# One core: the first products of two sequence blocks write half their planes straight into the sum, and the other half is added by accumulating DMA

## Chip, cores and metric

The kernel runs on one core of one Trainium2 chip. The metric is the device time of one execution in microseconds; the median of the runs of the kernel before is 262.36 (three runs, 262.0 to 262.48).

## What is computed

Inputs are bf16, the sequence has 2048 positions and 640 channels. `_A_ref` is a gated long convolution, `_B_ref` a SwiGLU feed-forward network with 1728 hidden units.

```python
def _A_ref(q, k, v, shift_k, ssm_k, ssm_D):
    # k_shift: sum over 4 taps of shifted k times shift_k
    kv = k_shift * v
    # y: causal convolution of kv with ssm_k over the 2048 positions, per channel
    y = y + kv * ssm_D
    return q * y

def _B_ref(x, w_gate, w_up, w_down):
    return (silu(x @ w_gate) * (x @ w_up)) @ w_down

h = x + _A_ref(layernorm(x), k, v, shift_k, ssm_k, ssm_D)
h2 = h + _B_ref(layernorm(h), w_gate, w_up, w_down)
```

## The kernel before

The sequence is cut into four blocks i of 512 positions. The convolution is done with a transform over 512 points with real and imaginary planes, written as matmuls against a table `ftab`. For each block of the filter, `kload` fetches it (`kc`), `ktrans` turns it on TensorE and evicts it to `KT`, and `kfwd` transforms it (L613) into even and odd parts (`C`, `R` and `KO`), which VectorE joins by a sum and a difference (`bfly`, L584). `kcomb` adds neighbours: on VectorE for C1 (L695), by accumulating DMA from GpSimd for the two others (L691).

For a block of the input, `kv` fetches k transposed (`kT`, a DMA transpose, L517) and v (`vt`), makes the shifted sum on TensorE (L715, L720), evicts it into `kT`, brings it back by five DMA transposes into `kvo`, and VectorE multiplies it into `vt` (L751). For block 0 the way back is by TensorE (L734, L739). `xfwd` transforms `vt` (L613; block 2 uses `quarters`, L650) into `X` and `FO`; `kvo` lies in the same bytes as `FO`, so the transposes into `kvo` wait until the last butterfly has read `FO`.

`prod(j, i)` multiplies the transform of input block j with filter part i - j and adds it to the sum `Y` of output block i. For each half f2 there are two multiplications over 2560 elements per partition (L826, L827), which write four planes into the ring `T` of five slots; one subtraction and one addition over 1280 elements (L832) make of them the real and the imaginary result. For j = 0 these two write `Y` itself; for j > 0 they write `T` and a third instruction adds that to `Y` (L843), except for the products (1,3) and (2,3), whose results go to `ZB` and are added to `Y` by a DMA that GpSimd issues (L840, `accum_op`). With j = i a last butterfly makes `IE` and `IO`. `IO` lies in the bytes of `vt`, so the next load of `vt` waits until the inverse transform has read `IO`.

`inverse(i)` transforms back (L907, four tiles of PSUM, two from `IO` and two from `IE`), and for each tile VectorE multiplies by the normalized q and forms a sum (L921, into `xh`), GpSimd scales it (L925), ScalarE forms the sum of squares (L927) and adds epsilon (L951), GpSimd takes the power -1/2 (L958), and ScalarE (L961, L963; VectorE, L966, in block 0) writes the normalized tile `qo`. A DMA transpose on SP's queue turns it into `hnT`. `ffn(i)` needs `hnT`: gate and up products are L1030 and L1031, or L988 in blocks 0 and 3, which work on halves of `hnT` and so start after two of the four transposes. ScalarE evicts both (L1006, L1008 or L1053, L1055; `GU`, `ub`), VectorE multiplies them (L1010, L1057); the down projection is L1093, with short remainders at L1105 and L1075. The results are added to `xh` (L1120, L1123, L1082) and stored.

PSUM is used as four units of two banks; a tile of matmuls waits until one is free, which is when an eviction (`evict`, L505 on ScalarE, L495 and L497 on VectorE) has read it. What order the instructions have on each of the five engines is written out by hand: `ORDER` lists the numbers of all tasks for each engine (a task is one instruction or one group of matmuls), `VECTOR` the evictions that VectorE takes instead of ScalarE, `FILL` some extra matmuls. `schedule` only fits the lists together and picks the PSUM units; each engine runs its list in order and waits on semaphores where a task needs another. So an instruction that waits holds back all that stands behind it on its engine.

Of the kernel before, what the change touches and what calls it, by code (L numbers as in the profile page):

```python
# [10 lines left out]
ALU = mybir.AluOpType  # L11
# [12 lines left out]
class _Task:  # L24
    __slots__ = ("eng", "fn", "cost", "lat", "deps", "after", "succ", "npred", "ready", "end", "start",
                 "opens", "tiles", "idx", "clock", "sem", "seq", "dma", "name", "gap", "lock", "fill", "late", "pause", "alt")
# [32 lines left out]
class _Graph:  # L59
# [38 lines left out]
    def add(self, eng, name, fn, cost, r=(), w=(), pr=(), pw=(), skip=(), lat=None, dma=None, after=(), lock=None):  # L98
        t = _Task()
# [11 lines left out]
        t.alt = None  # L111
        t.seq = len(self.tasks)
        for ap in r:
            for c in self.cells(ap):
                q = self.lastw.get(c)
# [3 lines left out]
        for ap in w:  # L119
            for c in self.cells(ap):  # L120
                q = self.lastw.get(c)
# [109 lines left out]
    def emit(self, block):  # L231
# [5 lines left out]
        for t in self.glob:  # L237
# [13 lines left out]
            for d in (t.deps | {t.pause} if t.pause is not None else t.deps):  # L251
                if d.eng == t.eng == "pe":
                    continue
                key = d.sem if d.dma is not None else d.eng
                val = 16 if d.dma is not None else d.idx
                merged.append((d, key, val))
# [13 lines left out]
            if t.dma is not None:  # L270
                t.sem = es.enter_context(nc.semaphore("s_d%d" % nd))
                nd += 1
                t.clock[t.sem] = 16
# [4 lines left out]
        for t in self.glob:  # L278
            if t.dma is not None and not t.succ:
                prog["sp"].append(lambda e, t=t: e.wait_ge(t.sem, 16))  # L280
# [49 lines left out]
    """,  # L330
    "dve": """
# [874 lines left out]
```

## Time and profile before

| | |
|---|---|
| median of 3 runs | 262.36 us |
| the profiled execution | 261.95 us |
| its span | 260.1 us |
| TensorE matmul busy | 253.6 us, 97% |
| VectorE busy | 203.3 us, 78%, 298 instructions |
| ScalarE busy | 188.4 us, 72% |
| GpSimd busy | 35.8 us, 14% |

All durations below come from that one execution; its time lies 1.85 us above its span, which is the time before the first and after the last instruction. In the profile PE is TensorE, PEld its weight loads, DVE is VectorE, ACT ScalarE, POOL GpSimd and SP the queue that issues most DMAs. A row of the timeline gives start, duration, engine, line, what is written from what, and in brackets how long the engine had stood idle and what ended that. Neighbouring instructions of an engine overlap a little, so that the distance from one start to the next is shorter than the duration. In the chain of waits each row is a piece of the chain of work that ended last. Matmuls overlap so much that PE shows as busy also where it is merely spread out; whether it waited is read from the distance between starts.

### The profile page before, as it was taken

How to read it: one execution, taken by the hardware profiler on the slowest of the kernel's cores; microseconds unless marked ns; L12 is line 12 of the kernel's file. 1: busy time of each engine (PE TensorE's matmuls, PEld its weight loads, DVE VectorE, ACT ScalarE, POOL GpSimd, SP SyncE). 2: the span in 40 equal slices, each digit the busy share in tenths (PEclk: the TensorE clock that was granted, in tenths of full speed). 3: DMA queues.
4: the chain of work that ended last, by engine and by line, in shares of the span. 5: the costliest groups of instructions: out<-in, count | busy, mean ns of one | idle time of the engine just before them, and what ended most of it. 6: DMA issues, size and time to landing. Idle time of an engine off the chain costs nothing.

```text
span 260.1 us, 4707 instructions
## 1 busy us (share of the span) xinstructions
PE 253.6 (97%) x1900; PEld 168.4 (65%) x1900; DVE 203.3 (78%) x298; ACT 188.4 (72%) x359; POOL 35.8 (14%) x53
## 2 busy tenths in 40 slices
PE   8999988899999999999999999999999999999996
PEld 6767545468888757644445667444456678888763
DVE  1799899999999999999999999999998131123214
ACT  2789999995996889668978697548698846745320
POOL 1000400401213033000040170311003202000000
DMA  6998964999999771630110064794500020300003
GB/s 186 327 346 223 326 161 84 227 317 217 228 135 178 96 195 28 151 126 5 40 20 0 12 154 104 177 215 89 103 1 0 4 50 25 79 0 3 25 3 126
DMA packets 44793, 31.13 MB, mean 120 GB/s; under 512 B 32354, under 2 KB 41443, under 8 KB 44771
## 3 DMA queue, kind: packets, MB, share of 16 engines
q1 hardware_dynamic: 41968, 25.58, 37.8%
q0 software_dynamic: 2144, 5.24, 11.7%
q8 instruction: 15, 0.25, 0.4%
q10 hardware_dynamic: 658, 0.01, 0.1%
q14 instruction: 8, 0.06, 0.1%
HBM read 15.69 MB, written 2.62 MB: 70 GB/s over the span
## 4 chain that ended last, share of the span: by engine, by line
PE 86%; ACT 6%; DVE 4%; DMA 2%; issue 1%; SPq 0%; DVEq 0%
PE ps L988 22%; PE ps L1093 20%; PE ps L1030 11%; PE ps L1031 11%; PE ps L613 7%; PE ps L907 6%; PE ps L720 3%; DMA kc<-in_A_ssm_k_dram 2%; ACT C L505 1%; PE ps L1075 1%; ACT KT L505 1%; PE ps L1105 1%; PE ps L715 1%; DVE xh L921 1%; ACT KO L505 1%; ACT X L505 1%
## 5 line engine op out<-in xcount | busy, mean ns | idle before, releaser
L1093 PE MATMUL ps<-Wd,GU 128*128 128x384 bf16 (+1 forms) x390 | 55.5, 299 | 0.0
L1093 PEld LDWEIGHTS ps<-Wd,GU 128*128 128x128 bf16 x390 | 37.9, 98 | 15.7 <-issue 0.9
L988 PE MATMUL ps<-hnT,GA 128*128 128x256 bf16 x140 | 31.1, 273 | 0.0
L988 PE MATMUL ps<-hnT,UA 128*128 128x256 bf16 x140 | 31.1, 273 | 0.0
L826 DVE TENSOR_TENSOR T<-X,C 128x2560 bf16<-128x2560 bf16 x20 | 29.7, 1485 | 0.2
L827 DVE TENSOR_TENSOR T<-X,C 128x2560 bf16<-128x2560 bf16 x20 | 29.7, 1483 | 0.1
L1010 DVE TENSOR_TENSOR GU<-GU,ub 128x512 bf16<-128x512 bf16 (+1 forms) x28 | 10.8, 401 | 21.3 <-ACT ub L1008 17.5
L988 PE MATMUL ps<-hnT,UB 128*128 128x256 bf16 x120 | 26.9, 273 | 0.0
L988 PE MATMUL ps<-hnT,GB 128*128 128x256 bf16 x120 | 26.9, 272 | 0.0
L1030 PE MATMUL ps<-hnT,GA 128*128 128x512 bf16 x70 | 26.5, 379 | 0.0
L1031 PE MATMUL ps<-hnT,UA 128*128 128x512 bf16 x70 | 26.5, 379 | 0.0
L1008 ACT ACTIVATE ub<-ps 128x512 bf16<-128x512 f32 (+2 forms) x32 | 17.0, 540 | 9.9 <-DVE GU L1010 3.8
L1006 ACT ACTIVATE GU<-ps 128x512 bf16<-128x512 f32 (+1 forms) x28 | 15.1, 562 | 10.8 <-PE ps L988 10.6
L1030 PE MATMUL ps<-hnT,GB 128*128 128x512 bf16 x60 | 22.8, 379 | 0.0
L1031 PE MATMUL ps<-hnT,UB 128*128 128x512 bf16 x60 | 22.7, 379 | 0.0
L613 PE MATMUL ps<-KT,ftab 128*128 128x320 bf16 x128 | 20.1, 300 | 1.4 <-ACT kT L505 0.6
L1053 ACT ACTIVATE GU<-ps 128x512 bf16<-128x512 f32 x26 | 15.1, 598 | 7.4 <-PE ps L1031 7.4
L1055 ACT ACTIVATE ub<-ps 128x512 bf16<-128x512 f32 (+1 forms) x30 | 16.8, 569 | 5.0 <-DVE GU L1057 4.0
L878 POOL TENSOR_TENSOR st<-st,half 128x8 f32<-128x8 f32 x4 | 9.6, 2400 | 74.9 <-ACT st L872 74.9
L921 DVE SCALAR_TENSOR_TENSOR xh<-ps,st,xh 128x640 bf16<-128x640 f32 x16 | 13.6, 880 | 6.8 <-PE ps L907 5.7
L927 ACT ACTIVATE qo<-xh,mv 128x640 bf16<-128x640 bf16 x16 | 13.3, 828 | 6.9 <-POOL mv L925 6.9
L613 PEld LDWEIGHTS ps<-KT,ftab 128*128 128x128 bf16 x128 | 10.8, 98 | 9.3 <-ACT KT L505 1.4
(108 smaller groups left out, 492.8 us busy)
## 6 DMA issues: line engine op xcount, KB each, us to landing
kc<-in_A_ssm_k_dram SPq DMA_DIRECT2D x4, 640.0 KB, 6.4
xh<-in_A_q_dram SPq DMA_DIRECT2D x4, 640.0 KB, 5.3
vt<-in_A_v_dram SPq DMA_DIRECT2D x4, 640.0 KB, 4.3
Y<-ZB POOLq DMA_DIRECT2D x4, 640.0 KB, 5.7
out_dram<-xh SPq DMA_DIRECT2D x15, 160.0 KB, 1.9
Wd<-in_B_w_down_dram SPq DMA_DIRECT2D x1, 1280.0 KB, 8.9
C<-C POOLq DMA_DIRECT2D x1, 1280.0 KB, 11.4
C<-R POOLq DMA_DIRECT2D x1, 1280.0 KB, 11.2
```

The source lines that it names most:

```text
L613: last = e.matmul(pt.f(c, W), ftab[:, cs, j, f * P:(f + 1) * P], src[:, j, c * W:(c + 1) * W], start=(j == par), stop=(j == par + 2))
L826: g.add("dve", nm, lambda e, x=x, k=k, t1=t1: e.tensor_tensor(out=t1, in0=x, in1=k, op=ALU.mult), cdve(2560), r=[x, k], w=[t1])
L827: g.add("dve", nm, lambda e, x=x, k=ksw, t2=t2: e.tensor_tensor(out=t2, in0=x, in1=k, op=ALU.mult), cdve(2560), r=[x, k], w=[t2])
L907: last = e.matmul(pt.f(c, W), itab[:, cs, f, j, :], src[:, j // 2 if len(fs) == 1 else f, cs, c * W:(c + 1) * W], start=(f == 0 and cs == ...
L921: g.add("dve", nm, lambda e, pt=pt, x2=x2, s=s, j=j, m=m: e.scalar_tensor_tensor(out=x2, in0=pt.f2(W), scalar=s[:, 3, j:j + 1], in1=x2, op ...
L988: last = e.matmul(pt.flat(M, a + M * k), w[:, c, f0:f0 + P], hnT[:, c, ts], start=(c == 0), stop=(c == NC5 - 1))
L1006: g.add("act", nm, lambda e, pt=pt, gv=gv, pg=pg: e.activation(out=gv, in_=pg(pt), func=ACTF.Silu, scale=gain), max(400, cact(n)), w=[gv], ...
L1008: g.add("act", nm, lambda e, pt=pt, uv=uv, pu=pu: e.activation(out=uv, in_=pu(pt), func=ACTF.Copy, scale=gain), max(400, cact(n)), w=[uv], ...
L1030: e.matmul(pt.f(0, N), wg[:, c, f0:f0 + P], hnT[:, c, :], start=(c == 0), stop=(c == NC5 - 1))
L1031: last = e.matmul(pt.f(1, N), wu[:, c, f0:f0 + P], hnT[:, c, :], start=(c == 0), stop=(c == NC5 - 1))
L1055: g.add("act", nm, lambda e, pt=pt, uv=uv, a=ps_u, ts=ts: e.activation(out=uv, in_=pt.f(a[0], N, a[1])[:, ts], func=ACTF.Copy, scale=gain) ...
L1093: last = e.matmul(pt.flat(c1 - c0, P + c0), slots[fb][:, at * P:(at + 1) * P], Wd[:, fb, c0:c1], start=(fb == 0 and not second), stop=(fb ...
```

## The change

Two products, (0,2) and (0,3), go through the function `planes`, which was there and was called by nothing. `YT` is one tensor over the bytes of `Y`, what lies between, and `T`, so that one instruction can write a plane into `Y` and its partner into `T`. Of each product half, the two multiplications (L823) write planes 0 and 2 (for odd i 1 and 2) into `Y` and the two others into `T`; one instruction negates one of them in `T` (L826 in the changed file, a `tensor_scalar` over 1280 elements); and GpSimd issues one accumulating DMA (L833) that adds the two planes in `T` to the two in `Y`, 2 x 1280 elements per partition. The subtraction and addition (L832 before) fall away. `VECTOR` changes: VectorE evicts one `KT` tile and two `KO` tiles at the start (before: two `KT` and one `R`), and two more tiles late, one `kT` of block 3 and one `X` of block 3. And `ORDER` is a new list for all engines: the whole program stands in another order.

```diff
-        BN, ..., ACC, EA, KD, RD, LA, RA, HALF, PL = ..., (0, 1, 2), (0, 3), ()
+        BN, ..., ACC, EA, KD, RD, LA, RA, HALF, PL, TK, TE = ..., (0, 1, 2), (0, 3), ((0, 2), (0, 3)), (), 'pool'
...
-        Y = sb("Y", S[6], [2, 2, 2, D])
...
-        T = sb("T", o, [NU, 2, D])
+        YT = sb("YT", S[6], [(T_END - S[6]) // 2])
+        Y = YT[:, 0:8 * D].rearrange("p (f c s d) -> p f c s d", f=2, c=2, s=2)
+        T = YT[:, (T_OFF - S[6]) // 2:(T_END - S[6]) // 2].rearrange("p (u f d) -> p u f d", u=NU, f=2)
...
         def at_big(off, *dims):
-            return bass.AP(BIG[:].tensor, BIG[:].offset + off // 2, [list(BIG[:].ap[0])] + [list(d) for d in dims])
+            b, at = (BIG, 0) if off < S[6] else (BZ, S[7]) if S[7] <= off < S[7] + SLOT else (YT, S[6])
+            return bass.AP(b[:].tensor, b[:].offset + (off - at) // 2, [list(b[:].ap[0])] + [list(d) for d in dims])
...
 VECTOR = """
-    36 59 83
+    33 85 87 710 758
 """
```

`TK` is empty, so the new branch in `kload` and `ktrans` is not taken. The function that is now called, for j = 0:

```python
un = [ring_t.pop(0) for _ in range(2)]
ring_t.extend(un)
a, b = (T_OFF + 2560 * v for v in un)
u = [a, yo[1], yo[0], b] if i % 2 else [yo[0], a, yo[1], b]
neg = u[0] if i % 2 else u[1]
# for each pair of planes: d = x * k over u[p], u[q]; after the first pair: z = -z on plane neg
sets = ((3, 0),) if i % 2 else ((1, 3),)
# for each set: accumulating DMA from GpSimd, Y += the two planes in T
```

Three places show what moved. On VectorE, in block 1's inverse transform, the product (0,2) stood in this order (`X_54` is the transform of block 0, `C_51` the filter part 2, `xh_73` block 1's tile):

```order
L826 TENSOR_TENSOR T<-X_54,C_51 128x2x2x640
L827 TENSOR_TENSOR T<-X_54,C_51 128x2x2x640
L1010 TENSOR_TENSOR gz<-gz,ub_78 64x256
L921 SCALAR_TENSOR_TENSOR xh_73,mv_107<-ps,st_1_106,xh_73 128x640
L832 TENSOR_TENSOR Y<-T 128x1280
L1010 TENSOR_TENSOR GU<-GU,ub_78 128x256
L826 TENSOR_TENSOR T<-X_54,C_51 128x2x2x640
L751 TENSOR_TENSOR vt<-vt,kvo 128x4x3x128
L751 TENSOR_TENSOR vt<-vt,kvo 128x4x2x64
L832 TENSOR_TENSOR Y<-T 128x1280 x2
L827 TENSOR_TENSOR T<-X_54,C_51 128x2x2x640
```

Now it stands so (L947 is what L921 was, block 1's tile is `xh_72`, L1036 was L1010, L775 was L751):

```order
L823 TENSOR_TENSOR YT<-X_54,C_51 128x2x2x640
L1036 TENSOR_TENSOR gz<-gz,ub_77 64x256
L826 TENSOR_SCALAR YT<-YT 128x1280
L947 SCALAR_TENSOR_TENSOR xh_72,mv_107<-ps,st_1_105,xh_72 128x640
L947 SCALAR_TENSOR_TENSOR xh_72,mv_109<-ps,st_1_105,xh_72 128x640
L823 TENSOR_TENSOR YT<-X_54,C_51 128x2x2x640 x2
L1036 TENSOR_TENSOR GU<-GU,ub_77 128x256
L947 SCALAR_TENSOR_TENSOR xh_72,mv_106<-ps,st_1_105,xh_72 128x640
L823 TENSOR_TENSOR YT<-X_54,C_51 128x2x2x640
L1036 TENSOR_TENSOR GU<-GU,ub_78 128x2x256
L826 TENSOR_SCALAR YT<-YT 128x1280
L947 SCALAR_TENSOR_TENSOR xh_72,mv_108<-ps,st_1_105,xh_72 128x640
```

The four L832 are gone, two negations have come, and the multiplications of the product have moved in among the four per-tile steps of the inverse transform, three of which stood ahead of them before. On GpSimd, in the same place, the accumulating DMAs stand between the steps of the second layer norm (L951 was L925, L984 was L958):

```order
L951 TENSOR_SCALAR mv_109<-mv_109 128x1
L951 TENSOR_SCALAR mv_107<-mv_107 128x1
L833 DMA YT<-YT 128x2x1280
L984 TENSOR_TENSOR mv_107<-mv_107,half 128x1
L951 TENSOR_SCALAR mv_106<-mv_106 128x1
L984 TENSOR_TENSOR mv_109<-mv_109,half 128x1
L833 DMA YT<-YT 128x2x1280
L951 TENSOR_SCALAR mv_108<-mv_108 128x1
L984 TENSOR_TENSOR mv_106<-mv_106,half 128x1
L984 TENSOR_TENSOR mv_108<-mv_108,half 128x1
```

Before there was no DMA in that stretch; in block 2 two more stand in the same way. On SP's queue, in block 1's `kv`, the table of the inverse transform was fetched ahead of the transposes into `kvo`:

```order
L512 DMA GA<-in_B_w_gate_dram 128x5x896
L512 DMA itab<-cst_itab 128x2048
L517 DMA_TRANSPOSE kvo<-kT 128x4x128
L512 DMA PK<-in_B_w_up_dram 128x5x64
L517 DMA_TRANSPOSE kvo<-kT 128x4x128
L512 DMA PK<-in_B_w_gate_dram 128x5x64
L517 DMA_TRANSPOSE kvo<-kT 128x4x128 x3
L512 DMA vt<-in_A_v_dram 128x2560
```

Now the table comes behind the first of these transposes, and other weights come earlier:

```order
L515 DMA Wd<-in_B_w_down_dram 64x640
L515 DMA xh_72<-in_A_q_dram 128x2560
L515 DMA GB<-in_B_w_gate_dram 128x5x768
L520 DMA_TRANSPOSE kvo<-kT 128x4x128
L515 DMA itab<-cst_itab 128x2048
L520 DMA_TRANSPOSE kvo<-kT 128x4x128 x4
L515 DMA vt<-in_A_v_dram 128x2560
```

The order of the rest has changed as follows where the steps below need it. On ScalarE, up to the eviction that frees the PSUM unit for the first inverse tile of block 0, there are now 7 `KT` and 1 short `kT` eviction where there were 6 and 2, with 32 of 640 elements and 4 long `kT` in both; the first long `kT` eviction of block 1 stands behind 7 `KT` evictions instead of 4. On TensorE, the first ten transposes of one filter block are now followed by ten of the other, instead of twenty and twenty. In block 2, the matmuls between the last tile of the inverse transform and the first gate product are 52 of the down projection, 32 transform matmuls of block 3 (L613 before) and 4 remainders; before, they were 78, 20 and 8. Both programs have the same matmuls in all.

More of the change, by code (lines that the diff above doesn't have):

```diff
@@ L25 @@
     __slots__ = ("eng", "fn", "cost", "lat", "deps", "after", "succ", "npred", "ready", "end", "start",
-                 "opens", "tiles", "idx", "clock", "sem", "seq", "dma", "name", "gap", "lock", "fill", "late", "pause", "alt")
+                 "opens", "tiles", "idx", "clock", "sem", "seq", "dma", "name", "gap", "lock", "fill", "late", "pause", "alt", "parts")
 class _Tile:
@@ L111, in add @@
         t.alt = None
+        t.parts = 1
         t.seq = len(self.tasks)
@@ L254, in emit @@
                 key = d.sem if d.dma is not None else d.eng
-                val = 16 if d.dma is not None else d.idx
+                val = 16 * d.parts if d.dma is not None else d.idx
                 merged.append((d, key, val))
@@ L272, in emit @@
                 nd += 1
-                t.clock[t.sem] = 16
+                t.clock[t.sem] = 16 * t.parts
                 prog[t.eng].append(lambda e, t=t: t.fn(e).then_inc(t.sem, 16))
@@ L279, in emit @@
             if t.dma is not None and not t.succ:
-                prog["sp"].append(lambda e, t=t: e.wait_ge(t.sem, 16))
+                prog["sp"].append(lambda e, t=t: e.wait_ge(t.sem, 16 * t.parts))
         @block.gpsimd
@@ L318 @@
     "act": """
[11 rows of a table removed]
[11 rows of a table added]
     """,
     "dve": """
[10 rows of a table removed]
[10 rows of a table added]
     """,
     "pool": """
-        8 6 5 7 10 11 9 151 209 195 216 212 202 198 219 205 134 135 339 417 401 409 420 393 412 396 404 528 613 605 597 621
-        616 608 624 600 771 776 781 786 732 822 825 806 809 814 830 817 833
+        10 8 6 7 5 11 9 151 216 195 209 198 202 212 219 205 134 135 339 417 401 563 404 393 420 567 409 396 412 528 621 742
+        624 613 746 605 616 597 608 600 771 776 781 786 732 806 830 822 825 833 809 814 817
     """,
     "sp": """
[3 rows of a table removed]
[3 rows of a table added]
     """,
@@ L451, in bass_sequential_preLN__ssm_conv_h3__swiglu_ffn__prompt_kernel @@
         o += 17920
+        GB_OFF = o
         GB = sb("GB", o, [NC5, FBK * P])
@@ L470, in bass_sequential_preLN__ssm_conv_h3__swiglu_ffn__prompt_kernel @@
         assert o + 576 <= SBB + 16481 - A0, o + 576
-        BN, DIRECT, D8, PT, BN2, ST, R4, PAIR, WARM, ACC, EA, KD, RD, LA, RA, HALF, PL = (0,), (), (), (0,), (), (0, 1, 2, 3), ('xf2',), True, 24, ((1, 3), (2, 3)), True, (2, 3), (), (1, 2, 3), (0, 1, 2), (0, 3), ()
+        BN, DIRECT, D8, PT, BN2, ST, R4, PAIR, WARM, ACC, EA, KD, RD, LA, RA, HALF, PL, TK, TE = (0,), (), (), (0,), (), (0, 1, 2, 3), ('xf2',), True, 24, ((1, 3), (2, 3)), True, (2, 3), (), (1, 2, 3), (0, 1, 2), (0, 3), ((0, 2), (0, 3)), (), 'pool'
         g = _Graph(nc, es)
@@ L558, in bass_sequential_preLN__ssm_conv_h3__swiglu_ffn__prompt_kernel, with move @@
               r=[wcol[:], ident[:]], w=[dl[:]])
+        box = {}
         def kload(m):
+            if m in TK:
+                q = sb("kq%d" % m, (GB_OFF, GB_OFF + 10240, kc23, kc23 + 5120)[m], [4, D])
+                tload("kTq%d" % m, q[:], A_ssm_k[:, N * m:N * (m + 1)], D, N, 2000)
+                def move(e, m=m, q=q):
+                    for c in range(4):
+                        last = e.dma_start(KT[m][32 * c:32 * c + 32, :, :], q[:, c, :])
+                        if c < 3:
+                            last.then_inc(box[m].sem, 16)
+                    return last
+                box[m] = g.add(TE, "kq%d" % m, move, 1800 if TE == "sp" else 4400, r=[q[:]], w=[KT[m][:]], dma=(2000, 0), lat=2000, lock=False)
+                box[m].parts = 4
+                return
             load("kc%d" % m, kc[m][:], A_ssm_k[:, N * m:N * (m + 1)].rearrange("(c p) s -> p c s", p=P), 655360)
         def ktrans(m):
+            if m in TK:
+                if m == 0:
+                    z = KT[0][0:1, 0, :]
+                    g.add("dve", "D", lambda e: e.tensor_tensor(out=z, in0=z, in1=drow[0:1, :], op=ALU.add), 410,
+                          r=[z, drow[0:1, :]], w=[z])
+                return
             for jj in range(2):
@@ L767, in bass_sequential_preLN__ssm_conv_h3__swiglu_ffn__prompt_kernel @@
         ZH = {(j, f): sb("ZH%d%d" % (j, f), S[k], [4, 2, D]) for j, f, k in ((1, 0, 7), (2, 0, 2), (2, 1, 4))}
-        BIG = sb("BIG", 0, [T_END // 2])
+        BIG = sb("BIG", 0, [S[6] // 2])
+        BZ = sb("BZ", S[7], [8 * D])
         def pair(u, v):
```

60 rows, old and new, of the table ORDER are left out of this document.

## Prediction

> **What bounds the kernel now.** I read the page first, then the stretches of the span, then the chain of waits in order of time, then the timelines of TensorE and SP's queue where the chain shows a wait.
>
> ```profile
> span 260.1 us, 4707 instructions
> PE 253.6 (97%) x1900; PEld 168.4 (65%) x1900; DVE 203.3 (78%) x298; ACT 188.4 (72%) x359; POOL 35.8 (14%) x53
> 10.00:20.00 10.00, 10.00 (x98) 6.25 (x96) 8.68 (x18) 9.11 (x15) 0.00 (x0) 1.00 1.06 316
> 20.00:30.00 10.00, 9.88 (x104) 6.91 (x104) 9.73 (x13) 9.59 (x16) 0.95 (x1) 1.00 0.89 238
> 30.00:40.00 10.00, 8.96 (x73) 4.51 (x73) 9.13 (x12) 9.81 (x14) 2.04 (x1) 1.00 0.74 217
> 150.00:160.00 10.00, 10.00 (x76) 6.89 (x75) 9.93 (x12) 8.89 (x19) 4.53 (x5) 1.00 0.60 136
> ```
>
> The columns after the stretch and its sum are PE, PEld, DVE, ACT and POOL. TensorE and VectorE both look full in the middle, so shares don't decide which one binds. The chain does. These are its rows around its last waits, some from the middle, and the end:
>
> ```profile
> 49.83 2.35 PE ps L613 x16
> ...
> 146.21 2.17 PE ps L907 x16
> ...
> 148.76 7.17 PE ps L1093 x52
> ...
> 156.96 3.53 PE ps L1093 x26
> 160.49 2.17 PE ps L613 x16
> ...
> 253.95 3.65 PE ps L1075 x26
> 257.62 0.48 DVE xh L1082
> ```
>
> From 49.83 to 257.62 every piece of the chain is TensorE, each beginning where the one before ends. The pace shows that this is work and not waiting: 26 down products take 3.53, 52 take 7.17. VectorE is full beside it, but nobody waits long for it there. So 207.8 of the 260.1 us are TensorE's own work, the change removes no matmul, and what it can win lies before 49.83; what it can lose lies anywhere. Before 49.83 TensorE did wait:
>
> ```profile
> 6.14 1.38 PE L571 MATMUL ps<-ident,kc 128*128 128x128 bf16 x20
> 7.71 1.31 PE L571 MATMUL ps<-ident,kc 128*128 128x128 bf16 x20 [0.19 <-DMA kc<-in_A_ssm_k_dram]
> 41.27 2.33 PE L907 MATMUL ps<-IO,itab 128*128 128x320 bf16 x16 [0.74 <-ACT KO L505]
> 49.83 2.35 PE L613 MATMUL ps<-vt,ftab 128*128 128x320 bf16 x16 [0.67 <-DVE vt L751]
> 43.63 0.34 SPq L512 DMA_DIRECT2D vt<-in_A_v_dram  x1
> 48.03 1.74 DVE L751 TENSOR_TENSOR vt<-vt,kvo 128x1536 bf16<-128x1536 bf16 x3
> vt<-in_A_v_dram SPq DMA_DIRECT2D x4, 640.0 KB, 4.3
> ```
>
> Block 0's inverse starts at 41.27, when ScalarE frees a PSUM unit. It reads `IO` until 43.44 (16 matmuls, 2.17), only then may `vt` be loaded over it (43.63), that lands about 4.3 later, at 47.9, and the multiplication starts at 48.03, just as VectorE gets there. Transform 1 follows at 49.83. So two things end together at 48.03: the load behind the inverse, and VectorE's queue.
>
> **VectorE's load.** Both multiplications stay. Of each of four halves the pair of L832 goes and a negation comes.
>
> ```profile
> L826 DVE TENSOR_TENSOR T<-X,C 128x2560 bf16<-128x2560 bf16 x20 | 29.7, 1485 | 0.2
> L832 DVE TENSOR_TENSOR Y<-T 128x1280 bf16<-128x1280 bf16 x16 | 12.8, 819 | 0.2
> 38.02 1.55 DVE L832 TENSOR_TENSOR Y<-T 128x1280 bf16<-128x1280 bf16 x2
> L966 DVE TENSOR_SCALAR qo<-xh,mv 128x640 bf16<-128x640 bf16 x4 | 1.8, 438 | 0.0
> L739 DVE TENSOR_TENSOR vt<-ps,vt 128x1024 bf16<-128x1024 f32 x2 | 2.4, 1220 | 0.5 <-PE ps L734 0.5
> ```
>
> A pair takes 1.47 to 1.55 (two in 1.55 with their overlap). No negation of this width is in the trace. The nearest row is a `tensor_scalar` of 640 elements in 0.44; at least that, at most the 0.82 of a two-input instruction of the same 1280 elements. I take 0.65, because twice the elements at 0.44 less the overlap comes out there. One half saves 1.5 less 0.44 to 0.82, so 0.7 to 1.1, and four save 2.7 to 4.2; I take 3.4. Two evictions come to VectorE late (by L739's row about 1.2 for 1024 elements and 0.8 for 640), so its sum falls by 0.7 to 2.2, 1.4 by my value. All of it lies after 90 us beside full TensorE: worth nothing on the path. The Trainium skill, "VectorE: DVE Perf Modes" (the table of modes), lets a one-input 16-bit instruction run at four elements a cycle where two inputs get two; by it the negation would be near 0.4, an estimate, and the saving 4.4; the trace before has no such row, and the path would not notice.
>
> **The start, where it can count.** The change puts another order there, with nearly the same work. ScalarE's queue up to the eviction that lets the inverse begin has one `KT` eviction more and one short `kT` less:
>
> ```profile
> 30.49 1.61 ACT L505 ACTIVATE kT<-ps 128x1024 bf16<-128x1024 f32 x2
> 35.51 0.72 ACT L505 ACTIVATE KO<-ps 128x640 bf16<-128x640 f32 x1
> 36.09 1.27 ACT L505 ACTIVATE KT<-ps 128x1280 bf16<-128x1280 bf16 x1
> 37.21 1.35 ACT L505 ACTIVATE C<-ps 128x640 bf16<-128x640 f32 x2
> ```
>
> From start to start a `KO` takes 0.58 and a `KT` 1.12; the short `kT` lies under the `KO`, about 0.5. That is +0.6. The queue starts about 0.65 earlier, since the first PSUM tile is full after 10 transposes of 0.065 instead of 20. So 41.27 comes out at 41.3. ScalarE stood idle 1.5 us between 10 and 40 (10 less 9.11, 9.59 and 9.81); if the new order took all of that away, it would be 39.8. VectorE holds the other end: ahead of the second `IO` it has half of L695 more (1.4), and one `IE` butterfly less (0.74); with its 0.8 us wait for GpSimd gone from there, `IO` is ready near 40.8, not before. So the inverse starts between 40.8 and 41.8, I take 41.3, `vt` lands at 47.9 as now, and the DVE queue, with one eviction traded for another of the same length, arrives no later. Transform 1 starts at 49.8: term 0, from -0.5 to +0.5.
>
> **Waits that the change adds.** Each half of the products now ends in a DMA that GpSimd issues and VectorE later waits for, when it writes those ring slots again and when the next product adds to `Y`.
>
> ```profile
> L840 POOL DMA_DIRECT2D Y<-ZB x4: 1191/1194/1261, 162.5 to 180.8; - x4
> DMA to landing us min/median/max: 5.6/5.7/6.5
> ```
>
> The same transfer took 1.2 to issue and 5.6 to 6.5 to land. Between the last write of (0,2)'s second half and the next use of its slots stand, on VectorE, one L921, one eviction, three L751, a multiplication, an L832 and three L1120: about 7 us. That covers 5.7 and is up to 0.7 short of 6.5 with the issue of GpSimd behind other work; a delay of that size on VectorE is hidden, because its next work for TensorE, the gate products of block 1, comes several us later than this point. On GpSimd the issue holds back one power (L958) of the second layer norm by 1.2 per DMA, behind which is `hnT`; that is priced with the rival below.
>
> The sum against the profiled execution: 261.95 + 0 (start) + 0 (VectorE, hidden) + 0 (waits, hidden) = 261.95. The median of the runs before is 0.4 above that execution, so the forecast for the median is 262.3. About 0.2%, 0.5 us, is what a measurement of this kernel can tell from no change.
>
> **Rivals.** *The start gains.* If ScalarE's idle 1.5 and VectorE's go, the inverse starts at 40.8 or earlier and transform 1 with it: 0.5 to 1.4 less, 261.0 to 261.9. For it: both engines' idle time there is real. Against: both ends at 48.03 must move together. Chance 0.17.
>
> *VectorE is what binds.* Then the time falls with its sum, by 0.7 to 2.2: 260.1 to 261.6. For it: 9.93 of 10 us in the stretch quoted. Against: the unbroken TensorE chain. Chance 0.08. This is the rule of the Trainium skill, "Perfetto Trace Analysis" (Identifying the Most-Contended Engine): judge TensorE by its weight loads and not by matmul time, and work on the engine with the highest share; here 65% against VectorE's 78%.
>
> *`hnT` of block 2 is late.* Block 2's gates need all four transposes.
>
> ```profile
> 154.19 5.54 SPq L517 DMA_TRANSPOSE hnT<-qo  x4
> DMA to landing us min/median/max: 2.6/2.6/2.6
> L517 SPq DMA_TRANSPOSE kvo<-kT x5: 1267/1938/3014, 72.5 to 79.4; - x5
> DMA to landing us min/median/max: 2.4/5.0/10.6
> ```
>
> Now the inverse ends at 148.38 and the last transpose is issued at about 158.3 and landed at 161.0, 12.6 later; the gates start at 162.66, 14.3 later. In the new order only 52 down products (7.17), 32 transform matmuls (4.34) and four remainders (0.38) stand between: 11.9. If the layer-norm chain still took 12.6, TensorE would wait 0.7; and the transposes lie beside two accumulating DMAs. The second pair of rows shows what that did at 72.5 to 79.4, beside L691's accumulating DMAs: up to 10.6 to land. Were all of that excess of 8 added, it would be 9 us. For the other side: the last tile now comes 4.6 us after the third, so ScalarE and GpSimd have less to do at once, and the chain of a single tile is short. The point is whether the chain from the last tile to the landing takes more than 11.9. I price it at 0.7 to 4, likely 2: 263.0 to 266.3, and 264.3 by the likely value. Chance 0.18.
>
> *`itab` is late.*
>
> ```profile
> 26.16 0.52 SPq L512 DMA_DIRECT2D itab<-cst_itab  x1
> itab<-cst_itab SPq DMA_DIRECT2D x1, 512.0 KB, 9.9
> ```
>
> The table now stands behind the first `kvo` transpose, which waits for the first `kT` eviction of block 1; three `KT` evictions more (3.4) less the earlier start put that at 33.2 instead of 30.49, done by 34.2, so the table is issued near 36. It landed after 9.9 in the crowd of weights at 26; `vt`'s 640 KB took 4.3. That is 40.3 to 46: anything over 5.3 us delays the inverse, by up to 4.6. Likely about 1.5: 263.8. Chance 0.12.
>
> **How the numbers follow.** No change 0.45; the two faster rivals 0.17 + 0.08 = 0.25; the two slower 0.18 + 0.12 = 0.30. The range must leave out at most 2 in 10: from 260.9 (the start's gain to its end of 1.4) to 264.8, which takes in the likely prices of both slow rivals and not their far ends. No change by itself would be 261.8 to 262.8.
>
> **What would show it.** Right: transform 1 (after the first L775) starts at 49.3 to 50.3, the inverse of block 0 at 40.8 to 41.8 and held by a `KO` eviction; the chain is TensorE alone from there to about 257.6; the negation takes 0.4 to 0.8 and the DMAs of L833 land in 5.6 to 6.5; VectorE's sum is 201 to 203. Wrong: a first inverse matmul that waits for the `itab` DMA; a gate product of block 1 or 2 that waits for a DMA from `qo`; a chain that passes through L833; or a start of transform 1 before 49, with the same 207.8 behind it.

## The result and the profile after

The changed kernel takes 265.05 us (median of 4 executions, 264.06 to 265.49), the kernel before 262.42 (4 executions, 262.0 to 262.48): 1.0096 times as long, with a 95% interval from 1.0078 to 1.0114. It is slower by 2.6 us, where no change was forecast and the range ended at 264.8. The profiled execution took 265.05. Its page begins:

```profile
span 263.0 us, 4695 instructions
PE 254.3 (97%) x1890; PEld 169.4 (64%) x1900; DVE 201.9 (77%) x296; ACT 188.4 (72%) x357; POOL 40.3 (15%) x57
```

TensorE's work is the same as before, and VectorE's sum fell by 1.4 us to 201.9, the value that the prediction took. So the loss isn't work. TensorE's timeline shows where it is (start, duration, line; in brackets the idle time before the row and what ended it):

```profile
41.30 2.35 PE L933 MATMUL ps<-IO,itab 128*128 128x320 bf16 x16
45.65 2.84 PE L637 MATMUL ps<-KT,ftab 128*128 128x320 bf16 x16
50.42 4.46 PE L637 MATMUL ps<-vt,ftab 128*128 128x320 bf16 x20 [1.92 <-DVE vt L775]
54.81 1.06 PE L744 MATMUL ps<-kT,dg 64*64 64x512 bf16 x16
```

The inverse of block 0 starts at 41.30, as forecast, but it was not a `KO` eviction that let it begin: the last one ahead of it ended at 40.93. TensorE's matmuls ahead of it ended at 41.22, and the second of VectorE's two butterflies that make `IO` at 41.24:

```profile
39.69 1.55 DVE L608 TENSOR_TENSOR IO<-YT 128x1280 bf16<-128x1280 bf16 x2
```

The weight loads of the inverse stood idle for 0.41 until then. Transform 1, the row at 50.42, starts 0.59 later than before (49.83), after 1.92 us of idle TensorE in place of 0.67. 0.55 of the longer idle time is that 16 matmuls of `KT` stand ahead of it, where there were 20. And the transform's first 20 matmuls take 4.39 us from start to start (50.42 to 54.81). The stretches around them show the granted clock, the number behind the matmul count:

```profile
50.00:51.00 1.00, 0.58 (x3) 0.62 0.86 191
51.00:52.00 1.00, 1.00 (x6) 0.50 0.04 7
52.00:53.00 1.00, 1.00 (x5) 0.50 0.80 157
53.00:54.00 1.00, 1.00 (x7) 0.67 0.47 76
```

It stood at half for 3.4 us (0.38 x 2 of the first stretch, two whole ones, 0.33 x 2 of the fourth) and was 1.00 again from there on. Before, it was 1.00 from the first to the last stretch. The chain of waits says what transform 1 waited for, and shows the only other hole behind it:

```profile
43.41 0.28 SPq L520
...
43.74 4.97 DMA vt<-in_A_v_dram
...
48.73 0.04 DVE vt L775
...
50.42 4.46 PE ps L637 x20
...
89.04 0.33 issue
89.37 2.88 PE ps L1119 x20
```

The load of `vt` was issued at 43.74 (43.63 before) but landed 5.0 later, at 48.71, in place of 4.1. VectorE had been free at 47.7 and waited 1.0. Directly ahead of the load on SP's queue stands a DMA transpose into `kvo` (L520), which was not there before:

```profile
42.04 1.65 SPq L520 DMA_TRANSPOSE kvo<-kT  x1
43.74 0.58 SPq L515 DMA_DIRECT2D vt<-in_A_v_dram  x1
```

The end, to be set beside the last row of the chain before (257.62, span 260.1):

```profile
260.31 0.48 DVE L1108 SCALAR_TENSOR_TENSOR xh<-ps,st,xh 128x256 bf16<-128x256 f32 x1 [0.80 <-PE ps L1101]
```

The account of the two profiled executions, 3.10 us apart (265.05 less 261.95):

| piece | before | after | lost |
|---|---|---|---|
| to the start of transform 1 | 49.83 | 50.42 | 0.59 |
| from there to the last VectorE instruction | 207.79 | 209.89 | 2.10 |
| from there to the end of the span (one decimal) | 2.5 | 2.7 | 0.2 |
| outside the span | 1.85 | 2.05 | 0.20 |

Of the 2.10, 1.57 is the lower clock (4.39 less the 2.82 that the same 20 matmuls take at full clock in two experiments below), and 0.33 the hole at 89.04, which the profile can't name; it ends 0.08 after VectorE's last `GU` product ended at 89.29. The remaining 0.20 shows in no row.

Two more rows answer to what the prediction named: the negation, and GpSimd's accumulating DMAs with their landing.

```profile
L826 DVE TENSOR_SCALAR YT<-YT 128x1280 bf16<-128x1280 bf16 x4 | 1.9, 486 | 0.0
```

```profile
L833 POOL DMA_DIRECT2D YT<-YT x4: 1241/1245/1269, 98.3 to 154.5; - x4
DMA to landing us min/median/max: 5.7/6.1/6.6
```

Nothing waited for these DMAs, neither VectorE nor a later transfer.

### The profile page after: what moved, and what is told of

It reads as the page before. It is cut to its first block, busy times and chain, and to the rows that moved or that the text cites. A ratio compares the mean times of both kernels' runs of the same rounds, so it can differ in the third digit from the quotient of the medians.

```text
span 263.0 us, 4695 instructions
## 1 busy us (share of the span) xinstructions
PE 254.3 (97%) x1890; PEld 169.4 (64%) x1900; DVE 201.9 (77%) x296; ACT 188.4 (72%) x357; POOL 40.3 (15%) x57
## 4 chain that ended last, share of the span: by engine, by line
PE 85%; ACT 8%; DMA 4%; issue 1%; DVE 0%; SPq 0%
PE ps L1014 22%; PE ps L1119 20%; PE ps L1057 11%; PE ps L1056 10%; PE ps L637 7%; PE ps L933 5%; PE ps L744 2%; DMA kc<-in_A_ssm_k_dram 2%; ACT C L508 2%; DMA vt<-in_A_v_dram 2%; ACT KT L508 2%; ACT KO L508 2%; PE ps L1101 1%; PE ps L1131 1%; PE ps L739 1%; ACT FO L508 1%
## 5 line engine op out<-in xcount | busy, mean ns | idle before, releaser
L1036 DVE TENSOR_TENSOR GU<-GU,ub 128x512 bf16<-128x512 bf16 (+1 forms) x28 | 11.0, 403 | 19.9 <-ACT GU L1032 13.7
L1056 PE MATMUL ps<-hnT,GA 128*128 128x512 bf16 x67 | 25.4, 379 | 0.0
L852 DVE TENSOR_TENSOR YT<-X,C 128x2560 bf16<-128x2560 bf16 x16 | 23.8, 1486 | 0.1
L853 DVE TENSOR_TENSOR YT<-X,C 128x2560 bf16<-128x2560 bf16 x16 | 23.8, 1486 | 0.1
L1056 PE MATMUL ps<-hnT,GB 128*128 128x512 bf16 x57 | 21.6, 379 | 0.0
L947 DVE SCALAR_TENSOR_TENSOR xh<-ps,st,xh 128x640 bf16<-128x640 f32 x16 | 13.9, 881 | 9.2 <-PE ps L933 9.2
L858 DVE TENSOR_TENSOR YT<-YT 128x1280 bf16<-128x1280 bf16 x24 | 19.4, 820 | 0.2
L904 POOL TENSOR_TENSOR st<-st,half 128x8 f32<-128x8 f32 x4 | 7.2, 1802 | 80.2 <-ACT st L898 80.2
L637 PE MATMUL ps<-vt,ftab 128*128 128x320 bf16 x96 | 16.4, 322 | 1.9 <-DVE vt L775 1.9
```

The source lines that it names most:

```text
L637: last = e.matmul(pt.f(c, W), ftab[:, cs, j, f * P:(f + 1) * P], src[:, j, c * W:(c + 1) * W], start=(j == par), stop=(j == par + 2))
L852: g.add("dve", nm, lambda e, x=x, k=k, t1=t1: e.tensor_tensor(out=t1, in0=x, in1=k, op=ALU.mult), cdve(2560), r=[x, k], w=[t1])
L853: g.add("dve", nm, lambda e, x=x, k=ksw, t2=t2: e.tensor_tensor(out=t2, in0=x, in1=k, op=ALU.mult), cdve(2560), r=[x, k], w=[t2])
L858: g.add("dve", nm, lambda e, p=p, q=q, d=d, op=op: e.tensor_tensor(out=d, in0=p, in1=q, op=op), cdve(1280), r=[p, q], w=[d])
L1056: e.matmul(pt.f(0, N), wg[:, c, f0:f0 + P], hnT[:, c, :], start=(c == 0), stop=(c == NC5 - 1))
```

## The experiments

**Theories.** A: the loss is in the start; `vt` lands late, TensorE stands idle for long, and the clock falls behind that. B: the accumulating DMAs, or the later order, cost the time. Against the kernel before, the line numbers of the changed kernel are shifted by 24 to 26; an experiment with an added line has them one higher than the kernel it comes from. Each kernel was timed beside the kernel before, whose medians there were 262.26 to 262.37.

**The changed kernel again** (`e0_after_again`, unaltered).

> The changed kernel, unaltered, profiled a second time. Theory A (start and clock: TensorE stands idle 1.9 us before transform 1, the granted clock falls after it, and these two are most of the loss) expects 264 to 265.5, transform 1 starting at 50 or later, and a mean clock below 1.00 wherever the time is near 265. Theory B (the accumulating DMAs of the products, or the order of the later work, cost the time) expects the same 264 to 265.5 also where the clock is 1.00, with a wait of TensorE after 90 us.

265.56 (263.87 to 267.09, 7 executions), 1.0098 times before (1.0063 to 1.0133). Idle before transform 1 was 2.01, `vt` landed after 5.1, and the clock was at half for 3.4 us from 51.2 on. Each execution has its mean clock: with the four of the result, 6 of 11 lie at 0.992 to 0.994, which is about what one drop of 3.4 us to half makes of 263 us, and take 265.05 to 267.09 (median 265.56); the other 5 lie at 0.999 or 1.00 and take 263.87 to 265.04 (median 264.12). So the drop comes in about half of the executions and is worth about 1.4; some 1.75 are lost without it, and there was no wait of TensorE after 90 us in this profile either.

**TensorE kept busy in the wait** (`e1_fill_wait`).

```diff
-FILL = "20:6 313:8"
+FILL = "20:6 313:8 354:18"
```

> The changed kernel with 18 extra matmuls of 192 columns (0.083 us each by the six at 15.51, 1.5 us together) put on TensorE ahead of transform 1, where it waits 1.92 us. Their results are overwritten. Theory A: the clock stays at 1.00 between 50 and 54 us, the first 20 matmuls of transform 1 take 2.7 us in place of 4.4, and the time falls by about 1.7 to 263.4. Rival: the clock falls for another reason (the whole of the slack stretch from 45 on, or the DMAs), and the time stays at 265.

263.89 (12 executions), 1.0049 (1.0027 to 1.0071): 1.67 less than the changed kernel beside it. TensorE's timeline:

```profile
48.93 1.65 PE L251 MATMUL ps<-ident 128*128 128x192 bf16 x18
51.01 2.89 PE L638 MATMUL ps<-vt,ftab 128*128 128x320 bf16 x20 [0.42 <-DVE vt L776]
53.83 1.06 PE L745 MATMUL ps<-kT,dg 64*64 64x512 bf16 x16
```

The fall is the 1.7 expected. The 20 matmuls take 2.82, and in none of the 12 executions was the mean clock below 0.999. Transform 1 is no earlier (51.01), so matmuls whose results are thrown away are worth 1.67 here. What brings the clock down is TensorE's idle time.

**The other way round** (`e7_before_idle`): in the kernel before, two `KT` tiles no longer fill the wait.

```diff
-        ... 120 94 102 100 128 350 ...
+        ... 120 94 102 350 100 128 ...
```

(That is TensorE's list; the two evictions, 101 and 129, move in the same way on ScalarE.)

> The kernel before with two KT tiles (8 matmuls, 1.1 us) moved from ahead of transform 1 to behind its first tile, so that TensorE stands idle 0.67 + 1.1 = 1.8 us there and nothing else of the start changes. If idle TensorE brings the clock down: half clock for about 3.4 us in part of the executions, 263.5 where it stays up (the 1.1 us of work that no longer fill the wait) and 265.2 where it falls. Rival (the clock in after falls for something else, such as the crowd of DMAs): 263.5 throughout, clock 1.00.

264.88 (6 executions), 1.0081 (1.0055 to 1.0107). Two executions at 0.999 and 1.00 take 263.44 and 263.72, four at 0.994 take 264.75 to 265.42: both numbers as expected. In the profile `vt` landed after 4.9 and the idle time was 2.28:

```profile
50.38 0.98 PE L614 MATMUL ps<-vt,ftab 128*128 128x320 bf16 x4 [2.28 <-DVE vt L752]
```

```profile
50.00:51.00 1.00, 0.62 (x4) 0.85 1.68 98
51.00:52.00 1.00, 1.00 (x6) 0.50 0.88 216
...
54.00:55.00 1.00, 1.00 (x9) 0.95 0.97 202
```

Again 3.4 us at half (0.3, three stretches, 0.1). The kernel has no new product and the same DMAs: idle time alone does it.

**The start of after, the rest of before** (`e6_start_after`): every engine's list is that of after up to the end of transform 1 and that of before from there, with the old products; `VECTOR` is `33 85 87`.

> The reverse: the order of after up to transform 1, then the order of before with the old products and no accumulating DMA for them. Theory A: the whole loss without the new products, 264 to 265.5, transform 1 at 50.4 or later after an idle TensorE of 1.9 us, the clock at half behind it in more than every second execution. Rival: 262.4, since products and later order are those of before.

264.14 (5 executions), 1.0072 (1.0052 to 1.0092). Three executions at clock 1.00 take 263.97 to 264.14, two at 0.994 take 264.55 and 265.01. Its transform 1:

```profile
50.62 4.39 PE L614 MATMUL ps<-vt,ftab 128*128 128x320 bf16 x20 [1.96 <-DVE vt L752]
```

So 1.8 of the 2.6 to 3.2 us are there without the new products and without the new later order. Theory A holds for the greater part; but drops came in two of five executions, fewer than it expected, and those without one are still 1.6 to 1.8 above before.

**The start of before, the rest of after** (`e5_start_before`), the same cut.

> The order of before up to transform 1 (all tasks that begin before it, with their evictions), then the order of after, with the new products. Theory A (the loss is in the start): transform 1 at 49.8, clock 1.00, and 262.0 to 262.9 in all. Rival: the later order with its accumulating DMAs loses too; then 263.5 or more with a start as before.

266.25 (4 executions), 1.0147 (1.0125 to 1.0168); theory A's 262.0 to 262.9 did not come. Transform 1 started at 49.87 and the clock was 1.00, yet TensorE then waited 0.70 for an `X` eviction, 1.03 for `ub` and 1.48 ahead of the first down product. The first two lie where the two orders were joined. It shows that the later order does not fit any start; how much it loses by itself it doesn't show.

**Order without new products** (`e3_order_alone`): the list of products that take the new form is empty, and each pair of multiplications gets its L858 pair back in VectorE's list.

```diff
-... HALF, PL, TK, TE = ..., ((0, 2), (0, 3)), (), 'pool'
+... HALF, PL, TK, TE = ..., (), (), 'pool'
```

> The order of after, with the old form of the two products in it (two multiplications, a subtraction, an addition, no DMA). Theory A: 264 to 265.5 like after, with the idle time before transform 1 and the lower clock behind it. Theory B: 262.4, since the DMAs are gone; or, if the shorter VectorE queue is what after needs, above 265.5 with waits for VectorE after 100 us.

267.31 (6 executions), 1.0169 (1.0130 to 1.0208), 1.75 above the changed kernel beside it: above 265.5, with waits for VectorE, as the last clause expected. VectorE and TensorE's waits, from the page and the waits:

```profile
PE 254.3 (95%) x1890; PEld 168.6 (63%) x1900; DVE 206.1 (77%) x300; ACT 188.6 (71%) x357; POOL 33.1 (12%) x53
```

```profile
PE ps L638 <- DVE vt L776: 3.9, 2, 2.4
PE ps L675 <- DVE vt L776: 0.6, 1, 0.6
```

The 2.4 is transform 1; the other 1.5 and the 0.6 are waits of blocks 3 and 2 for their `vt`, which VectorE multiplies late, with 4.2 us more to do than in the changed kernel. In this order the saving of the new products is needed: they are a gain of some 1.7 that only mends what the order would lose.

**New products in the old order** (`e2_planes_alone`): `ORDER` and `VECTOR` of before, with the new instructions where the old ones stood. Of VectorE's list, (0,2):

```diff
-        560 561 293 392 562 290 564 516 518 563 566 565 517 568 567 302 569 ...
+        560 562 293 392 561 290 564 516 518 566 565 517 568 570 302 298 307 569 ...
```

> The order of before with the new form of the products (0,2) and (0,3) put into it: the multiplications, negations and accumulating DMAs stand where the instructions they replace stood, as near as the ring slots allow. Theory A: no change, 262.0 to 262.9, VectorE's sum about 200 (203.3 less 4 x 1.06), start as before. Theory B: the accumulating DMAs make VectorE wait (the first product of (1,2) needs the landed sum), and TensorE behind it: 264 or more.

272.45 (5 executions), 1.0369 (1.0342 to 1.0397). VectorE's sum is 199.7, as expected, but VectorE waited for the accumulating DMAs, and TensorE for `hnT` of block 2 (us in total, times, the longest):

```profile
DVE YT L853 <- DMA YT<-YT: 8.6, 3, 4.1
...
PE ps L1058 <- DMA hnT<-qo: 4.1, 1, 4.1
```

SP's queue and the landings between 155 and 171 show why:

```profile
158.98 9.88 SPq L521 DMA_TRANSPOSE hnT<-qo  x4
```

```profile
YT<-YT POOLq DMA_DIRECT2D x2, 640.0 KB, 7.8
...
hnT<-qo SPq DMA_TRANSPOSE x4, 6.3
```

Four transposes beside two accumulating DMAs (issued at 157.55 and 159.62) took 2.5 us each to issue and 6.3 to land (medians). In the changed kernel it was 1.24 and 2.7: the DMAs were issued at 150.47 and 154.48, and only the first transpose, at 155.3, lay wholly beside one (6.1); the others, from 159.3 on, took 2.6 to 2.7. Around the 4.1 us of idle TensorE (it ended at 171.21) the clock was at half from 170 or earlier to 176.3. What theory B says of the accumulating DMAs is right of this order and wrong of the changed one: there the distance between DMA and user had been made.

**The `kvo` transpose early** (`e4_kvo_early`, and profiled again as `e10_kvo_early_again`), in the changed kernel:

```diff
-PE   ... 320 316 114 128 118 120 104 124 324 116 ...
+PE   ... 320 316 324 114 128 118 120 104 124 116 ...
-ACT  ... 71 321 317 115 150 123 129 121 119 105 125 117 99 95 325 97 ...
+ACT  ... 71 321 317 325 115 150 123 129 121 119 105 125 117 99 95 97 ...
```

> The changed kernel with the third part of block 1's shifted sum (4 matmuls, L739) and its kT eviction moved ahead of ten KT evictions, as it stands in before, so that the last kvo transpose is no longer issued right ahead of the load of vt. Theory V (the transpose still in flight is what makes the load land after 5.0 us in place of 4.1): it lands after 4.1 again; the inverse begins up to 0.5 later, because the eviction now lies ahead of the one that lets it begin; transform 1 starts 0.4 to 0.9 earlier than in after, the idle time before it falls below 1.5, the clock stays at 1.00 there, and the time is 262.6 to 263.6. Rival: the landing stays at 4.9 to 5.4 (another cause), and the time stays at 265 or grows by the 0.5.

> The changed kernel with the early kvo transpose, profiled a second time for the same landing. Theory V: 4.1 again, transform 1 near 50.0. By chance alone: 4.9 to 5.4 is as likely. In either case TensorE waits for UB in block 0's gate products and for block 0's evictions ahead of the down products, if the end of this order is set there and not by the start of transform 1: 263.7 to 264.2.

263.87 (263.67 to 264.23, 5 executions, all at clock 1.00), 1.0053 (1.0034 to 1.0072); the second profile's execution took 263.28. From the landings and the timeline of the first:

```profile
vt<-in_A_v_dram SPq DMA_DIRECT2D x1, 640.0 KB, 4.1
```

```profile
44.18 0.35 SPq L516 DMA_DIRECT2D vt<-in_A_v_dram  x1
49.98 2.89 PE L638 MATMUL ps<-vt,ftab 128*128 128x320 bf16 x20 [0.98 <-DVE vt L776]
52.80 1.06 PE L745 MATMUL ps<-kT,dg 64*64 64x512 bf16 x16
```

The load lands after 4.1 (4.2 in the second), transform 1 starts at 49.98 (49.64), the idle time is 0.98 and the clock stays up. The time doesn't come back to 262.4, and 263.87 lies above the 262.6 to 263.6 expected: TensorE now waits 0.69 (0.63) ahead of the first down product, and in the first profile 0.42 for the weights `UB`. Against the five executions of the changed kernel without a drop (median 264.12) this kernel is only 0.25 faster, so nearly all that the early landing wins is that the clock stays up.

**The `kvo` transpose late, in the kernel before** (`e8_before_kvo_late`): on SP's list `326` goes behind `323 322`, directly ahead of `315`, the load; `324` and `325` go late on TensorE and ScalarE.

> The kernel before with the third part of block 1's shifted sum and its kT eviction moved late, behind the KO eviction that lets the inverse begin, so that the last kvo transpose is issued right ahead of the load of vt, as in after; nothing else changes. Theory V (a transpose in flight makes the load land late, every time): the landing is 4.9 or more in place of 4.1, the inverse starts up to 0.5 earlier, transform 1 at 50.0 to 50.7, the time 262.6 to 263.5. Rival (the landing falls at 4.1 or 4.9 by chance, as two runs with the start of before suggest, 4.9 and 5.1 without such a transpose): the time spreads as that of before does, with a median of 262.4 or less.

263.43 (12 executions), 1.0050 (1.0021 to 1.0078). SP's queue and the landing:

```profile
42.14 1.60 SPq L518 DMA_TRANSPOSE kvo<-kT  x1
43.78 0.58 SPq L513 DMA_DIRECT2D vt<-in_A_v_dram  x1
```

```profile
vt<-in_A_v_dram SPq DMA_DIRECT2D x1, 640.0 KB, 5.3
```

Transform 1 started at 50.90, a little later than expected. Nine executions at full clock take 263.00 to 263.66, three at 0.993 take 265.18 to 265.82. One moved transpose makes 1.1 us of loss in the kernel before, clock drops included.

**The kernel before again** (`e9_before_again`, unaltered).

> The kernel before, unaltered, profiled a second time for the landing of vt. If the landing varies by chance: 4.1 with a time near 262.1, or 4.9 to 5.1 with a time near 263.3 and transform 1 at 50.4. Theory V alone expects 4.1.

262.36, with `vt` landed after 3.9 and transform 1 at 50.09. Over all profiles: with a transpose issued directly ahead, the load landed after 4.9, 4.9, 5.0, 5.1, 5.3 and 5.4 (six of six); without, after 3.9 to 4.2 in eight of ten, and after 4.9 and 5.1 in two with the start of before. So the transpose makes the late landing regular; what makes it in those two is open.

**Three places mended** (`e11_three_mended`): the early transpose, and

```diff
-DVE  ... 385 386 278 282 387 ...
+DVE  ... 385 278 386 282 387 ...
-SP   ... 692 913 903 906 916
+SP   ... 692 903 913 906 916
```

> The changed kernel with the new products and three places of its order mended: the early kvo transpose, one of block 0's gate products (GU) on VectorE ahead of the butterfly that makes IO of block 1, so that ScalarE can free PSUM for the down products earlier, and one store of 640 columns ahead of the next to last store. If the account is complete (late landing with the clock behind it, 0.6 to 0.7 at the first down product, 0.15 after the last matmul): vt lands after 4.1, clock 1.00, no wait of TensorE for the first down product, and 262.4 to 262.9, no more than 0.2% above before. If something else in the later order costs time: 263.3 to 263.9, as with the early transpose alone.

264.02 (10 executions, all at 0.999 or 1.00), 1.0057 (1.0038 to 1.0077). The expectation failed. `vt` landed after 4.0 and 2.83 us lay after the start of the last matmul, as before (2.84; 3.01 in the changed kernel), but TensorE waited 0.83 ahead of the first down product. The chain of waits no longer passed through transform 1; it went through VectorE, from 51.95 on nearly without a break:

```profile
50.11 1.81 POOL mv L985
51.95 0.45 DVE qo L993
52.40 0.73 DVE YT L859
...
84.29 1.47 DVE YT L870
85.78 0.43 DVE GU L1037
86.20 0.73 DVE IO L609
87.31 0.39 ACT ub L1035
87.86 2.22 PE ps L1120 x15
```

**Less work for VectorE** (`e12_mended_less_dve` in that kernel, `e13_before_less_dve` in the kernel before):

```diff
-lambda e, x=x, k=ksw, t2=t2: e.tensor_tensor(out=t2, in0=x, in1=k, op=ALU.mult)
+lambda e, x=x, k=ksw, t2=t2, q=64 if (j, i, f2) == (1, 1, 1) else D: e.tensor_tensor(
+    out=t2[:, :, :, 0:q], in0=x[:, :, :, 0:q], in1=k[:, :, :, 0:q], op=ALU.mult)
```

> The three-times mended kernel with one multiplication of the product (1,1) (second half) cut from 640 to 64 channels, so that VectorE has about 1.3 us less to do before the first down product; the rest of that product is left out. Theory D (in the new order VectorE, busy without a break from 52 to 87 us, sets the start of block 0's down products, and that is the loss that remains): the wait of 0.83 of TensorE before the first down product is gone and the time falls by 0.8 to 1.2, from 264.0 to about 263.0. Rival (the start of the kernel alone is what remains; the wait is made up later): 263.8 to 264.1, no change.

> The kernel before with the same multiplication cut in the same way. In its order two tiles of block 1's inverse stand ahead of the down products and TensorE waits nowhere after 50 us, so 1.3 us less on VectorE should bring nothing: 262.2 to 262.5. If VectorE binds in that order too, 261.0 to 261.5.

The mended kernel: 264.01 (8 executions), 1.0071 (1.0044 to 1.0098), no change; its wait fell from 0.83 to 0.50, and the chain goes through the start again:

```profile
44.34 4.13 DMA vt<-in_A_v_dram
...
50.18 2.89 PE ps L638 x20
...
86.81 0.55 PE ps L1018 x5
87.36 0.50 issue
87.86 2.88 PE ps L1120 x20
```

The kernel before: 262.26 against 262.26, 1.0001 (0.9987 to 1.0014). So in the order of before 1.3 us of VectorE's work are worth nothing. In the new order VectorE is nearly level with TensorE at 87 us, and the two chains fit that whichever comes later sets the end; that VectorE alone makes the remaining loss is not borne out.

**What stays open.** The profile of `e12_mended_less_dve` (263.43) can be reckoned up against the second one of before (262.36): 0.09 at the start, about 0.8 between transform 1 and the last matmul (0.50 of it the wait at the down product), 0.2 outside the span. But the medians of the mended kernels, near 264.0, lie 0.6 above this, and their executions at full clock spread from 262.4 to 265.0. Where that comes from no profile shows. Nor do the pieces add up: the start of after alone costs 1.8 (`e6_start_after`), the changed kernel with that start mended still 1.5 to 1.75 (`e4_kvo_early`, the two mended kernels), and both together 2.6 to 3.2. So the greater part of what is lost at full clock is located only in part.

## Why the prediction was wrong

**The start.** The number of its first half came out, by luck: the inverse was to start at 41.3 (the sum given, 41.27 + 0.6 - 0.65, is 41.2) and did at 41.30, but ScalarE's `KO` eviction, whose queue the sum follows, did not hold it. VectorE's `IO` was ready at 41.24, where the prediction had 40.8, and in the four profiles with the early transpose the first inverse matmul waits 0.29 to 0.30 for `IO`. Over the nine profiles with this start it was 41.30 to 41.96, inside the 40.8 to 41.8 but for three values up to 0.16 outside. The step that failed in the time is the next: "I take 41.3, `vt` lands at 47.9 as now". It landed at 48.71. The prediction had noted that the first `kvo` transpose is held by a later `kT` eviction and followed what that does to `itab`; it did not follow the last one of the five, whose eviction went behind ten evictions of filter tiles, and which so came to stand directly ahead of the load. That makes the landing 0.9 us later, shown in both directions by moving the one transpose.

**A term that was missing.** The prediction had no term for the clock. A later start of transform 1 was priced by its delay alone, at most 0.5, and in the profiled execution a delay of 0.59 brought another 1.57 with it. Of the five executions without a drop four lie below 264.8, the end of the range, and of the six with one none does. Idle time before transform 1, as the one profiled execution of each run shows it, and the executions with a drop (mean clock up to 0.994):

| kernel | idle, us | with a drop |
|---|---|---|
| after, filled | 0.42 | 0 of 12 |
| before | 0.67 | 1 of 79 |
| after, early transpose; three mended | 0.98, 1.07; 0.90 | 0 of 6; 0 of 10 |
| three mended, less VectorE work | 1.02 | 2 of 8 |
| before, late transpose | 1.51 | 3 of 12 |
| after | 1.92, 2.01 | 6 of 11 |
| start of after; before, tiles moved | 1.96; 2.28 | 2 of 5; 4 of 6 |
| after's order, old products | 2.38 | 2 of 6 |

The Trainium skill, "TensorE: Matmul & The Clock Gate" (Part 1, What's actually happening), describes a free-running window of 3413 ns, with half clock after at least one idle window and full clock again after at least one busy one. The half clock of 3.4 us, and a drop in some executions of one kernel and not in others, agree with such a window. Its section "Why this matters for your kernels" asks only for no gap above about 3 us; here gaps of 1.9 to 2.4 were enough, and the measurement decides. Those are the gaps of the five profiled executions with a drop behind transform 1's wait. Where it begins is open: in the profiles the clock stayed at 1.00 behind 1.43 us (`e2_planes_alone`), 1.48 (`e5_start_before`, ahead of the down product) and 1.51, and the drops in the rows at 1.02 and 1.51 came in executions that were not profiled, so their own idle time isn't known.

**VectorE's load.** The sum of 201.9 lies in the 201 to 203 forecast. The negation took 0.49 where 0.65 was taken (bounds 0.44 to 0.82); the reason given for 0.65 does not carry it, since twice 0.44 less the overlap of 0.09 (two of 0.82 in 1.55) is 0.79. With 0.49 the same sum gives 201.3, so that it came out at exactly 201.9 is luck. The Trainium skill, "VectorE: DVE Perf Modes" (the table of modes), had given near 0.4 as an estimate, the nearer of the two. That VectorE's saving is worth nothing on the path is right of the order of before, shown by 1.3 us less work and no change. It isn't right of the new order, which without the new products (4.2 us more on VectorE) takes 1.75 more.

**The added waits.** Right within 0.1: landing 5.7 to 6.6 (forecast 5.6 to 6.5), and nobody waited. They are hidden by the distance that the new order gives them; at the old places VectorE waits 9.7 us in all (the 8.6 shown, and 1.1 at the other multiplication).

**The rivals.** *The start gains*: no. *VectorE is what binds*: not in the order of before. *`itab` is late*: issued at 35.86 as forecast, landed after 3.9, at 39.8, 1.5 before it was needed. *`hnT` of block 2 is late*: not in the changed kernel, whose first gate product of block 2 (167.18) follows the transform without a gap; but the mechanism is real, 4.1 us in the old order, at the upper end of its price, and the clock comes on top. The slower side was given 0.30, for two mechanisms that didn't act.

**Smaller terms that were counted as zero.** 0.33 ahead of the first down product, which in the new order directly follows the last gate product, where before three tiles of the inverse (24 matmuls; the expectation of `e13_before_less_dve` says two) stood between; 0.2 after the last VectorE instruction; 0.2 outside the span.

## What to carry to other kernels

When the order on a DMA queue changes, look for every load on the path at what is issued directly ahead of it, not only at when it is issued itself: one transpose there made a landing 0.9 us later. Price a wait of TensorE not by its length alone but with the lower clock behind it, surely from about 2 us on and perhaps from less, and put the work or even thrown-away matmuls into it. A rewritten operation and its order belong together: the new products alone lost 10 us, the order alone 4.9, both together 2.6 to 3.2.

## What the runs showed of the hardware that was not expected

- In five profiles the granted clock falls to half after 1.9 to 2.4 us of idle TensorE, for 3.4 us; kernels whose profile shows such a gap have the drop in a third to two thirds of their executions; 18 matmuls of 192 columns in the gap kept it at 1.00 in 12 of 12.
- A load of 640 KB lands after 4.9 to 5.4 us with a DMA transpose issued directly ahead of it on the queue, and after 3.9 to 4.2 without, in eight of ten profiles.
- DMA transposes beside accumulating DMAs took 6.3 us to land (median of four), against 2.7.
- All nine profiled executions with the new products spend 2.03 to 2.10 us outside the span, the seven without them 1.80 to 1.86, whatever their order. Why four more accumulating DMAs (or what goes with them) cost 0.2 us there was not tried.
